# One input load of a fused attention and expert kernel moved from one DMA queue to another, another issued later

## The chip, the cores and the metric

The kernel runs on one core of a Trainium2 chip. The metric is the device time of one execution in microseconds (us); runs are compared by their medians. The profile is that of one execution; its span runs from the first to the last instruction and is shorter than the device time of the same execution.

## The reference

Two steps in a row. First an attention over 8 batches, 8 heads, 576 positions and 64 columns a head, in which each position sees itself and the 63 before it; then an expert layer with a gate, on 4608 tokens of 512 columns, with 1536 hidden columns.

```python
scores = scale * np.matmul(q, k.transpose(0, 1, 3, 2))
mask = (rel >= 0) & (rel < window)              # rel: query position less key position; window 64
scores = np.where(mask, scores, -1000000000.0)
attn = exp(scores - max) / (sum + 1e-09)
x = np.matmul(attn, v)                          # heads put side by side: 4608 x 512
gate = np.maximum(x @ w_gate, 0.0)
val = x @ w_val
out = (gate * val) @ w_out
```

Inputs and output are float32 in device memory.

## The kernel before

Everything is computed in 16-bit floats with float32 sums. Weights stay on the chip. The tokens are cut into nine tiles of 512; each tile is attended, turned so that columns lie on partitions, sent through gate and value matmuls and then through the output matmul. From the second tile on the expert products are made in Strassen's manner, with sums of weight blocks (`us`, `vs`) that VectorE and GpSimd form early in the run.

The program has two parts. `second_part` holds all but the opening. It is laid out by a planner (`Plan`), which gives each operation a key and estimated costs and writes one fixed order of instructions for each engine when the program is built; on the chip nothing is reordered. The planner's numbers, its assumed start times of the engines among them, are constants in the code. `first_part` is written out by hand. It brings the first windows of batch 0 through attention and starts the weights. The engines run in parallel, each in its own order, and wait for one another by semaphores.

What the opening does, in its order:

- Batch 0's q and k are loaded in four pieces, each of four heads: `heads_of(b, name, hh)` is the view with 128 rows (4 heads x 32 row groups) of 1152 values, `hh` 0 or 1 the half of the heads. "First" below means `hh` = 0, "second" `hh` = 1.
- First k and first q come as float32 over SyncE's DMA queue (L452, in the page `q1 hardware_dynamic`) into scratch that later holds `vs` (L450). They are then rounded to 16 bits into `nat[name, 0]` by `rounded` (L473 to L475): half of the columns by VectorE, half by ScalarE.
- Second k and second q come over GpSimd's DMA queue (`qk_load`, L386; in the page `q0 software_dynamic`), which rounds in flight: source float32, destination 16 bits.
- GpSimd then builds an identity and the band mask (`bands`, L356 to L368: two memsets, four selects), and issues three loads of v (`v_load`, L395) and four of weights (`w_part`, L376), all over q0. Later it copies parts of v (L512) and goes on with weights.
- VectorE fills constants, makes the additive `bias` from the mask (L471), and turns each of the four pieces into `kT` or `qT` by a transpose of 32x32 blocks (`qk_trans`, L392), in the order first k, first q, second k, second q. Then it copies parts of v (L512), takes reciprocals (L532), norms (L437) and turns (L442) the first tokens into `xt`.
- TensorE runs `PADS` small matmuls on zeros (L463), moves the mask into the score banks (L481, L487), one filler on zeros (`keep_hot`, L492), the scores of the first heads (L424), two more fillers, the scores of the second heads, the values (L430), and then the first expert matmuls (L836), which belong to `second_part`. ScalarE takes the exponentials (L504).

Of the kernel before, what the change touches and what calls it, by code (L numbers as in the profile page):

```python
# [10 lines left out]
FP32 = mybir.dt.float32  # L11
# [283 lines left out]
def kernel(  # L295
# [10 lines left out]
    nc = tc.nc  # L306
# [24 lines left out]
    def sb(name, shape, dt=FP16):  # L331
        return persist.tile([128] + shape, dt, name=name)

    wg, wv, wo = sb("wg", [NC, DF]), sb("wv", [NC, DF]), sb("wo", [NF, DM])
    us, vs = sb("us", [4, 2, 128 * HF]), sb("vs", [4, 2, 128 * HF])
# [3 lines left out]
    nat = {(name, hh): sb(f"{name}{hh}", [S // 32 * D]) for name in "kq" for hh in range(2)}  # L339
# [16 lines left out]
    def bands():  # L356
        nc.gpsimd.memset(mask, 1.0)
        nc.gpsimd.memset(ident, 1.0)
        for band, lo, hi in ((ident, 0, 0), (mask, 64, -1)):
            n = band.shape[1]  # L360
            nc.gpsimd.affine_select(
                out=band, in_=band, compare_op=mybir.AluOpType.is_ge, fill=0.0,
                base=lo, pattern=[[1, n]], channel_multiplier=-1,
            )
            nc.gpsimd.affine_select(
                out=band, in_=band, compare_op=mybir.AluOpType.is_ge, fill=0.0,
                base=hi, pattern=[[-1, n]], channel_multiplier=1,
            )  # L368

    def v_fixed(i, eng):  # L370
        eng.memset(v16s[i][:, :, :, D:VW].bitcast(FP32), ONE_ONE)
        eng.memset(v16s[i][0:64, 0].bitcast(FP32), 0.0)

    def w_part(wt, src, f0, f1, a):
        ns = slice(128 * f0, 128 * f1)
        nc.gpsimd.dma_start(wt[:, 2 * a:2 * a + 2, ns], src.rearrange("(a p e) n -> a p e n", a=2, e=2)[a, :, :, ns])  # L376
# [4 lines left out]
    def heads_of(b, name, hh):  # L381
        src = (q if name == "q" else k)[b, G * hh:G * hh + G]
        return src.rearrange("h (i j) d -> (h i) (j d)", i=32)

    def qk_load(b, name, hh):
        nc.gpsimd.dma_start(nat[name, hh], heads_of(b, name, hh))  # L386

    def qk_trans(b, name, hh):
        src = nat[name, hh].bitcast(FP32).rearrange("p (j e) -> p j e", e=32)
        dst = qTs[b % 2][:, hh] if name == "q" else kTs[b % 2][:, hh, 64:64 + S]  # L390
        dst = dst.bitcast(FP32).rearrange("p c o -> p (c o)")
        nc.vector.transpose(dst.rearrange("p (i j) -> p j i", i=32), src)  # L392

    def v_load(b, g, lo, hi):
        nc.gpsimd.dma_start(v16s[b % 2][lo:hi, g, :, 0:64],  # L395
                            v[b, :, 64 * g - 64 + lo:64 * g - 64 + hi].rearrange("h p d -> p h d"))

    def v_rows(b, uu):
        t = v16s[b % 2]
        up = {0: (0, 3), 1: (4, 5), 2: (6, 7)}[uu]  # L400
        down = {0: (2, 3), 1: (4, 5), 2: (6, 9)}[uu]
        return ((t[64:128, up[0]:up[1]:2], t[0:64, up[0] + 1:up[1] + 1:2]),
                (t[0:64, down[0]:down[1]:2], t[64:128, down[0] - 1:down[1] - 1:2]))
# [29 lines left out]
    def blocks_of(to, n):  # L433
        return to[:, 0:n * VW].rearrange("p (s c) -> p s c", c=VW)
# [12 lines left out]
    def first_part():  # L447

        n = S // 32 * D
        t32 = {name: vs.rearrange("p a k n -> p (a k n)").bitcast(FP32)[:, n * i:n * i + n] for i, name in enumerate("kq")}  # L450
        for name in "kq":
            nc.sync.dma_start(t32[name], heads_of(0, name, 0))  # L452
        for name in "kq":
            qk_load(0, name, 1)
        nc.vector.memset(zero, 0.0)
        nc.vector.memset(warm, 0.0)
        nc.scalar.activation(warm[:, 1:2], warm[:, 0:1], ACT.Exp)
        for i in range(2):
            v_fixed(i, nc.vector)
        nc.vector.memset(zero32, 0.0)  # L460
        bands()
        for _ in range(PADS):
            nc.tensor.matmul(banks[5][0:32, 0:16], zero[0:32, 0:32], zero[0:32, 0:16], start=True, stop=True, skip_group_check=True)  # L463
        for part in ((1, 0, 128), (3, 0, 128), (5, 0, 128)):
            v_load(0, *part)
        for a in range(2):
            for wt, src in ((wg, moe_w_gate), (wv, moe_w_val)):
                w_part(wt, src, 0, 4, a)
        for kT in kTs:
            nc.vector.memset(kT[:, :, 0:64], 0.0)  # L470
        nc.vector.tensor_scalar(bias, mask, 30000.0, -30000.0, MUL, ADD)  # L471

        def rounded(name, first, second):  # L473
            for i, copy in enumerate((first, second)):
                copy(nat[name, 0][:, n // 2 * i:n // 2 * (i + 1)], t32[name][:, n // 2 * i:n // 2 * (i + 1)])  # L475

        st = banks[0:4], banks[4:8]
        rounded("k", nc.vector.tensor_copy, nc.scalar.copy)
        for s in range(2):
            for g in range(G):  # L480
                nc.tensor.matmul(banks[6 + s][32 * g:32 * g + 32, 0:128], bias[:, 32 * s:32 * s + 32], ident,  # L481
                                 start=True, stop=True, skip_group_check=True)
        for s in range(2):
            nc.scalar.copy(biasT[:, s], banks[6 + s][:, 0:128])
        for u in range(2):
            for g in range(G):
                nc.tensor.matmul(st[u][g][:, 0:2 * U].rearrange("p (n c) -> p n c", c=64), ident,  # L487
                                 bias[:, None, :].to_broadcast([128, 2 * UB, 64]),
                                 start=True, stop=False, skip_group_check=True)

        def keep_hot(to):
            nc.tensor.matmul(to, zero32[:, 0:128], zero32[:, 0:2 * U], start=False, stop=False, skip_group_check=True)  # L492

        keep_hot(st[1][3][:, 0:2 * U])
        qk_trans(0, "k", 0)
        rounded("q", nc.scalar.copy, nc.vector.tensor_copy)
        qk_trans(0, "q", 0)
        for name in "kq":
            qk_trans(0, name, 1)
        for hh in range(2):  # L500
            for u in range(2):
                score_run([x[:, U * hh:] for x in st[u]], [(w, hh) for w in range(UB * u, UB * u + UB)], True)
                for g in range(G):
                    nc.scalar.activation(ps[4 * u + g][:, UB * hh:UB * hh + UB].rearrange("p n c -> p (n c)"),  # L504
                                         st[u][g][:, U * hh:U * hh + U], ACT.Exp, scale=scale)
            if hh == 0:
                for _ in range(2):
                    keep_hot(st[0][0][:, 0:2 * U])

        def copies(uu, copy, h0, h1):  # L510
            for to, at in v_rows(0, uu):
                copy(to[:, :, h0:h1, 0:64], at[:, :, h0:h1, 0:64])  # L512

        def values(u, hh):
            for i in range(UB):
                for s in range(2):
                    value_block(banks[2 * u + hh], VW * (2 * i + s), ps[4 * u:4 * u + 4], UB * u + i, hh, UB * hh + i, s)

        for hh in range(2):
            copies(0, nc.vector.tensor_copy, G * hh, G * hh + G)  # L520
            values(0, hh)
        nc.tensor.matmul(banks[2], zero[:, 0:128], zero, start=True, stop=True, skip_group_check=True)
        copies(1, nc.gpsimd.tensor_copy, 0, H)
        for hh in range(2):
            values(1, hh)
        SB = 2 * UB

        def x_of(u, hh):
            return xw[:, SB * (2 * u + hh):SB * (2 * u + hh) + SB]

        def recip(u, hh):
            nc.vector.reciprocal(rw[u][:, SB * hh:SB * hh + SB], blocks_of(banks[2 * u + hh], SB)[:, :, D:D + 1])  # L532

        def norm_of(u, hh):
            norm(banks[2 * u + hh], SB, x_of(u, hh), rw[u][:, SB * hh:SB * hh + SB])

        recip(0, 0)
        norm_of(0, 0)
        turn(xs[0], 0, 0, x_of(0, 0))
        recip(0, 1)  # L540
        norm_of(0, 1)
        for hh in (1, 0):
            recip(1, hh)
        for s in range(SB):
            nc.scalar.activation(x_of(1, 1)[:, s], blocks_of(banks[3], SB)[:, s, 0:D].rearrange("p (c e) -> p e c", e=2),
                                 ACT.Copy, scale=rw[1][:, SB + s])
        turn(xs[0], 1, 0, x_of(0, 1))
        norm_of(1, 0)
        for hh in range(2):
            turn(xs[0], hh, U, x_of(1, hh))  # L550
# [621 lines left out]
    with tc.manual_schedule():  # L1172
        first_part()
        PLANS.append(second_part())
# [30 lines left out]
```

## Time and profile before

| | |
|---|---|
| median of 3 runs | 307.1 us (304.96, 307.1, 308.22) |
| profiled execution, device time | 305.09 us |
| its span | 303.1 us |
| mean granted TensorE clock | 0.997 |
| busy: TensorE, VectorE, ScalarE, GpSimd | 294.5, 252.6, 213.1, 231.5 us |
| moved over q0 (GpSimd's DMA queue) | 18.29 MB, 46672 packets, 51.6% of the 16 DMA engines' span |
| moved over q1 (SyncE's and others' DMA queue) | 13.80 MB, 12720 packets, 14.5% |

The busy share of each engine in 40 slices of 7.6 us (a digit is tenths) shows how TensorE is less than full only in the first two slices and the last:

```profile
PE   7799999999999999999999999999999999999994
POOL 8698757999997999799558976699559567948630
DMA  7999999992599916933979835343931112001024
```

In names of the page PE is TensorE, PEld its weight loads, DVE VectorE, ACT ScalarE, POOL GpSimd, SP SyncE. The opening on GpSimd, in order of time (start, length, operation; an arrow in brackets names the idle time before and what ended it):

```profile
1.32 0.75 POOL L386 DMA_DIRECT2D k<-in_k_dram  x1 [0.80 <-POOLq L1189]
2.05 0.55 POOL L386 DMA_DIRECT2D q<-in_q_dram  x1
2.59 0.18 POOL L357 MEMSET mask<- 128x64 f16 x1
...
3.89 0.24 POOL L365 TENSOR_SCALAR_AFFINE_SELECT mask<-mask 128x64 f16<-128x64 f16 x1
4.07 2.80 POOL L395 DMA_DIRECT2D v<-in_v_dram  x3
6.85 0.70 POOL L376 DMA_DIRECT2D wg<-in_moe_w_gate_dram  x1
```

A DMA's row on an engine is the issue alone; the data lands later. The time to landing is listed for each issue in another view, from the issue's start.

### The profile page before, as it was taken

The numbers are of one execution on the slowest core, as the hardware profiler recorded it, in microseconds if no ns is written. First come the engines' busy times: TensorE is split into PE (matmuls) and PEld (weight loads), VectorE is DVE, ScalarE is ACT, GpSimd is POOL, SyncE is SP. The second block draws the span as 40 slices with busy tenths as digits, with TensorE's granted clock in tenths as the row PEclk, the third lists the DMA queues.
The fourth block names the chain that finished last, engine by engine and source line by source line (L and its number), as shares of the span: only waits on it lengthen the run. The fifth ranks groups of instructions, "written<-read, shape, count | busy, mean of one in ns | idle before, by whom it ended". The sixth has DMA issues, their size and how long they took to land.

```text
span 303.1 us, 11292 instructions
## 1 busy us (share of the span) xinstructions
PE 294.5 (97%) x4793; PEld 242.5 (80%) x4793; DVE 252.6 (83%) x428; ACT 213.1 (70%) x415; POOL 231.5 (76%) x233
## 2 busy tenths in 40 slices
PE   7799999999999999999999999999999999999994
PEld 5576655778767888888888888888888888888884
DVE  5879999999967988998869998889978688776962
ACT  4464426898588788785866987977588858887731
POOL 8698757999997999799558976699559567948630
PEclk9999999999999999999999999999999999999998
DMA  7999999992599916933979835343931112001024
GB/s 216 186 190 205 196 193 218 182 200 44 37 151 155 165 45 83 145 41 53 207 167 114 116 54 98 76 86 36 118 92 38 40 37 69 2 0 37 19 75 151
DMA packets 59586, 32.87 MB, mean 108 GB/s; under 512 B 39440, under 2 KB 54416, under 8 KB 59536
## 3 DMA queue, kind: packets, MB, share of 16 engines
q0 software_dynamic: 46672, 18.29, 51.6%
q1 hardware_dynamic: 12720, 13.80, 14.5%
q8 instruction: 37, 0.61, 0.9%
q14 instruction: 13, 0.11, 0.1%
q10 hardware_dynamic: 144, 0.07, 0.1%
HBM read 37.75 MB, written 9.44 MB: 156 GB/s over the span
## 4 chain that ended last, share of the span: by engine, by line
PE 89%; DMA 7%; DVE 1%; issue 1%; POOL 1%; ACT 0%; SPq 0%; ACTq 0%; DVEq 0%; POOLq 0%
PE bank L924 46%; PE bank L1088 21%; PE bank L998 6%; PE bank L789 5%; PE bank L430 4%; DMA q<-in_q_dram 3%; PE bank L424 2%; DMA v<-in_v_dram 2%; PE bank L836 2%; DMA v<-v 2%; PE bank L416 2%; DVE qT L392 0%; DVE v L512 0%; POOL k L386 0%; POOL v L395 0%
## 5 line engine op out<-in xcount | busy, mean ns | idle before, releaser
L958 POOL TENSOR_TENSOR g_sb<-pr,pr 128x512 f16<-128x512 f32 x96 | 121.1, 1277 | 37.8 <-ACT pr L949 9.1
L940 DVE TENSOR_TENSOR pr<-bank,pr 128x512 f32<-128x512 f32 x144 | 92.4, 680 | 20.2 <-PE bank L924 15.1
L933 ACT COPY pr<-bank 128x512 f32<-128x512 f32 x144 | 80.8, 590 | 23.1 <-PE bank L924 20.6
L924 PE MATMUL bank<-xt,us 128*128 128x256 f16 x384 | 56.1, 273 | 0.1
L924 PE MATMUL bank<-xt,vs 128*128 128x256 f16 x384 | 55.7, 273 | 0.0
L949 ACT ACTIVATE pr<-pr 128x512 f32<-128x512 f32 x72 | 44.9, 638 | 4.7 <-DVE pr L940 4.5
L684 ACT ACTIVATE p<-bank 128x512 f16<-128x512 f32 (+1 forms) x68 | 36.4, 591 | 10.0 <-PE bank L424 9.9
L924 PE MATMUL bank<-xt,wg 128*128 128x256 f16 x288 | 42.8, 273 | 0.1
L924 PE MATMUL bank<-xt,wv 128*128 128x256 f16 x288 | 42.8, 273 | 0.0
L924 PEld LDWEIGHTS <-vs 128*128 128x128 f16 x384 | 37.3, 98 | 5.3
L924 PEld LDWEIGHTS <-us 128*128 128x128 f16 x384 | 36.8, 98 | 5.1 <-issue 0.3
L395 POOL DMA_DIRECT2D v<-in_v_dram x40 | 35.1, 881 | 1.5 <-DMA wo<-in_moe_w_out_dram 1.1
L1088 PEld LDWEIGHTS <-g_sb 128*128 128x128 f16 x336 | 32.5, 98 | 3.9
L1088 PE MATMUL bank<-wo,g_sb 128*128 128x256 f16 x252 | 32.6, 273 | 0.0
L971 ACT ACTIVATE pr<-bank 128x512 f32<-128x512 f32 x48 | 27.5, 602 | 6.1 <-PE bank L924 4.8
L924 PEld LDWEIGHTS <-wv 128*128 128x128 f16 x288 | 27.7, 98 | 4.5
L924 PEld LDWEIGHTS <-wg 128*128 128x128 f16 x288 | 27.7, 98 | 4.1 <-DVE xt L442 0.4
L437 DVE TENSOR_TENSOR xw<-bank,r 128x448 f16<-128x448 f32 (+2 forms) x45 | 25.8, 574 | 1.6
L1088 PEld LDWEIGHTS <-ss 128*128 128x128 f16 x252 | 24.5, 98 | 3.0
L442 DVE STREAM_TRANSPOSE xt<-xw 128x512 f16<-128x512 f16 (+2 forms) x38 | 24.9, 669 | 0.4
L998 PE MATMUL bank<-wo,g_sb 128*128 128x512 f16 x96 | 23.9, 380 | 0.0
L1088 PE MATMUL bank<-ts,ss 128*128 128x256 f16 x168 | 21.8, 273 | 0.0
(103 smaller groups left out, 388.3 us busy)
## 6 DMA issues: line engine op xcount, KB each, us to landing
out_dram<-pr SPq DMA_DIRECT2D x35, 256.0 KB, 2.8
k<-in_k_dram POOLq DMA_DIRECT2D x15, 288.0 KB, 6.5
q<-in_q_dram POOLq DMA_DIRECT2D x15, 288.0 KB, 6.9
v<-in_v_dram POOLq DMA_DIRECT2D x32, 128.0 KB, 5.3
v<-v SPq DMA_DIRECT2D x12, 132.0 KB, 2.7
v<-v SPq DMA_DIRECT2D x24, 66.0 KB, 3.4
wg<-in_moe_w_gate_dram POOLq DMA_DIRECT2D x6, 256.0 KB, 6.6
wv<-in_moe_w_val_dram POOLq DMA_DIRECT2D x6, 256.0 KB, 8.7
```

The lines of the kernel that those rows point to most:

```text
L395: nc.gpsimd.dma_start(v16s[b % 2][lo:hi, g, :, 0:64], v[b, :, 64 * g - 64 + lo:64 * g - 64 + hi].rearrange("h p d -> p h d"))
L437: nc.vector.tensor_tensor(x, blocks_of(to, n)[:, :, 0:D].rearrange("p s (c e) -> p s e c", e=2), r[:, :, :, None].to_broadcast([128, n, 2, ...
L442: nc.vector.transpose(xt[:, 2 * hh:2 * hh + 2, c0:c0 + n].rearrange("p e (s c) -> p s e c", c=32), x)
L684: nc.scalar.activation(pp[g][:, 0:n].rearrange("p n c -> p (n c)"), st[g][:, 0:64 * n], ACT.Exp, scale=scale)
L924: nc.tensor.matmul(slot[to][:, HT * m:HT * m + HT], w[:, kk, 128 * m:128 * m + 128], x[:, kk], start=(first and m == 0 and kk == 0), stop= ...
L933: lambda e, hold=hold, slot=slot: nc.scalar.copy(hold["x"], slot["A"]),
L940: nc.vector.tensor_tensor(hold["x"], slot[to], hold["x"], ADD)
L949: lambda e: nc.scalar.activation(hold["x"], hold["x"], ACT.Relu), after=[o])
L958: lambda e: VEC[e].tensor_tensor(gh[:, fs:fs + 2, h], pair(a["x"]), pair(b["x"]), MUL),
L971: lambda e, hold=hold, slot=slot, i=i: nc.scalar.activation(hold["x"], slot["A"], ACT.Copy if i else ACT.Relu),
L998: nc.tensor.matmul(bank["b"][:, 0:c1 - c0], gs[t % 2][:, f, 128 * sub:128 * sub + 128], wo[:, f, c0:c1], start=(j == 0 and i == 0), stop=( ...
L1088: nc.tensor.matmul(bank[to][:, HD * m:HD * m + HD], a[:, f, 128 * m:128 * m + 128], b[:, f], start=(first and m == 0 and f == 0), stop=(f ...
```

## The change

First q no longer goes over SyncE's queue as float32 and through the rounding on VectorE and ScalarE. GpSimd loads it with `qk_load(0, "q", 0)`, straight into `nat["q", 0]` in 16 bits, as its first load, ahead of second k. The load of second q, `qk_load(0, "q", 1)`, is issued by GpSimd behind the six instructions of `bands` instead of ahead of them, still before the v loads. First k is loaded and rounded as before, without the helper. Planner, constants and `second_part` are the same.

```diff
     def first_part():
 
         n = S // 32 * D
-        t32 = {name: vs.rearrange("p a k n -> p (a k n)").bitcast(FP32)[:, n * i:n * i + n] for i, name in enumerate("kq")}
-        for name in "kq":
-            nc.sync.dma_start(t32[name], heads_of(0, name, 0))
-        for name in "kq":
-            qk_load(0, name, 1)
+        k32 = vs.rearrange("p a k n -> p (a k n)").bitcast(FP32)[:, 0:n]
+        nc.sync.dma_start(k32, heads_of(0, "k", 0))
+        qk_load(0, "q", 0)
+        qk_load(0, "k", 1)
         nc.vector.memset(zero, 0.0)
...
         nc.vector.memset(zero32, 0.0)
         bands()
+        qk_load(0, "q", 1)
...
-        def rounded(name, first, second):
-            for i, copy in enumerate((first, second)):
-                copy(nat[name, 0][:, n // 2 * i:n // 2 * (i + 1)], t32[name][:, n // 2 * i:n // 2 * (i + 1)])
-
         st = banks[0:4], banks[4:8]
-        rounded("k", nc.vector.tensor_copy, nc.scalar.copy)
+        for i, copy in enumerate((nc.vector.tensor_copy, nc.scalar.copy)):
+            copy(nat["k", 0][:, n // 2 * i:n // 2 * (i + 1)], k32[:, n // 2 * i:n // 2 * (i + 1)])
...
         qk_trans(0, "k", 0)
-        rounded("q", nc.scalar.copy, nc.vector.tensor_copy)
         qk_trans(0, "q", 0)
```

## The prediction

> **What bounds the kernel now.** I read the page first: TensorE is busy for 294.5 of 303.1 us, so it is the bound, and only its idle time can move the end. Stretches of 8 us put that idle time in two places: 2.15 us (0 to 8) and 1.64 us (8 to 16) before the first expert matmuls, then 0.69 us (40 to 48), 0.17 (48 to 56), 0.09 (64 to 72) and nothing until the last stores. The change edits only the part before 14.5 us, so I followed the chain of waits there:
>
> ```profile
> 1.32 0.74 POOL k L386
> 2.05 8.29 DMA q<-in_q_dram
> 10.35 0.02 issue
> 10.37 1.26 DVE qT L392
> ...
> 11.70 0.29 DVE v L512
> ...
> 13.84 0.59 DVE xt L442
> 14.43 0.04 issue
> 14.47 1.48 PE bank L836 x16
> ```
>
> Columns: start, length, what. The opening ends last on the load of the second q (issued 2.05, landed 10.35), its transpose, the copies of v, norm and turn. From 14.47 TensorE hardly stops, so a shift of that point shifts the end. I then asked how the four loads share the transfer engines, by the queue table of two windows (packets, MB, share of 16 engines), 2 to 5 us and 5.2 to 7.9 us:
>
> ```profile
> q1 hardware_dynamic: 233, 1.00, 93.9%
> ```
>
> ```profile
> q0 software_dynamic: 241, 0.52, 104.5%
> q1 hardware_dynamic: 24, 0.06, 5.6%
> ```
>
> First SP's queue q1 (k and q as f32) has the engines alone, then Pool's q0 takes over without a gap. Issue start plus time to landing gives k first heads 0.82+4.2 = 5.02, q first 1.26+5.1 = 6.36, k second 1.32+6.5 = 7.82, q second 2.05+8.3 = 10.35, the three v parts 4.07+7.0 = 11.07, 4.99+6.6 = 11.59 and about 12.24 (Pool's copy begins at 12.27). So this is one stream, and the loads land in order, about 1.4 us each. The last takes 2.5; the window 8 to 9.1 us shows what came between:
>
> ```profile
> q0 software_dynamic: 959, 0.16, 188.6%
> q8 instruction: 1, 0.02, 5.1%
> ```
>
> One instruction packet holds 5.1% of 16 engines for 1.1 us, so one engine for 0.9 us. The DVE timeline (start, length) shows where compute meets the stream:
>
> ```profile
> 6.86 0.45 DVE L475 CAST q<-vs 128x576 f16<-128x576 f32 x1
> 7.41 1.26 DVE L392 STREAM_TRANSPOSE qT<-q 128x576 f32<-128x576 f32 x1
> 8.52 1.24 DVE L392 STREAM_TRANSPOSE kT<-k 128x576 f32<-128x576 f32 x1
> 10.37 1.26 DVE L392 STREAM_TRANSPOSE qT<-q 128x576 f32<-128x576 f32 x1 [0.62 <-DMA q<-in_q_dram]
> ```
>
> DVE already waits 0.62 us for the stream before the last transpose. Further on the stream touches TensorE again (list of TensorE's weight-load waits: us in total, times, longest):
>
> ```profile
> PEld L789 <- DMA wv<-in_moe_w_val_dram: 0.3, 1, 0.3
> ...
> PEld L836 <- DMA wg<-in_moe_w_gate_dram: 0.3, 1, 0.3
> ```
>
> The weights arrive just in time, so a later stream is a later end, one for one.
>
> **The change, part by part.**
>
> *Rounding of q removed.* ACT loses 0.67 us (6.43 to 7.10): its next work is the first exponential at 9.13, after a wait of 2.02 for TensorE, so this is worth nothing by itself. DVE loses 0.45: the first q transpose can follow the first k transpose at about 7.05 instead of 7.41, the first scores start at 8.36 instead of 8.72, and the second k transpose ends 0.36 earlier. There the gain ends: the last transpose waits for the second q, and DVE's idle 0.62 becomes about 1.0. Worth 0 while that load lands near 10.4; without that cover it would be -0.36.
>
> *SP's second issue removed* (0.42 us). SP does nothing more until the store at 50.35: 0.
>
> *First q through Pool.* Same bytes read, half written. Price from two stretches of one us: 429 GB/s written by f32 packets (4 to 5 us, so 429 read), 208 GB/s written by rounding packets (7 to 8 us, so 416 read). 589.8 kB take 1.375 or 1.418 us: +0.04 in the stream. Measured landings bound it: 6.36-5.02 = 1.34 for f32 against 7.82-6.36 = 1.46 rounded, +0.12. I take +0.1. Pool issues it where it issued the second k before (1.32, 0.75 long, the first one's length), so k second takes the slot at 2.07, and the masks keep their 2.59 to 4.13.
>
> When do its packets begin? Before, none of q0 moved until about 5.1, as q1 had the engines. The nearest row with idle engines is the k load issued at 69.19, whose first bytes move at 70.48, 1.3 us later; with the first issue 0.15 longer that makes 2.8. The last of the first k's packets begin by about 4.3, 0.7 before it lands, so the queue would be ready in time: the low end is a gap of 0. The high end is 5.1, the earliest that the trace shows for this place: one more load stands behind 5.1 than before, +1.4. I take 2.8, since issue length plus 0.7 us also fits v loads on idle engines (74.00: 0.95 long, first bytes 1.66 after). The Trainium skill, "DMA: Bandwidth & Descriptors", section "Queues, rings and completion order", says that an engine takes turns between its queue rows, packet by packet. By that rule the missing q0 packets before 5.1 mean that they were not ready, and the sum would be the +1.4. The trace speaks more for order of arrival: the store issued at 97.96 behind Pool's backlog took 5.7 us to land, against a median of 2.8.
>
> *Second q behind the masks.* Its issue moves from 2.05 to 4.07 (0.55 long). Ready 0.7 after its end, 5.3, while the stream frees for it only about 7.5 (0.35 before k second lands, 7.86): 2.2 us of cover. On Pool it is moved past memsets and selects, which do not slip, as two issues still precede them; but three v issues and four weight issues behind it slip by 0.55. The third v is issued by 7.4, ready 8.1, needed some 0.6 (v spacing) twice after the second q's bytes, not before 9.5. The last weight issue ends at 10.2 instead of 9.64, where Pool waits 2.63 us for v anyway. All hidden; with the cover gone at most 0.55. DVE needs the mask as before (4.16).
>
> *The sum.* k first 5.02, q first 6.46, k second 7.92, q second 10.45 (the instruction packet still ahead of its end), v parts 11.17 and 11.69. Last transpose 10.47 to 11.73, copies 11.80, first expert matmuls 14.57: **+0.1 us**, and the weights that end TensorE's waits at 15.97 and 18.27 are as much later. Span 303.2; outside the span lie 305.09-303.1 = 1.99, so 305.2 for the profiled execution. That run stands 2.0 below the median of 307.1 (runs 304.96 to 308.22); on the median the forecast is 307.2.
>
> **The rivals.**
>
> *Late first packets (slower).* Place: the engines between the end of k first, about 4.3, and the first rounding packet. From 4.3 on every us costs one, up to +1.4: 308.5. For it: no q0 packet before 5.1. Against: 1.3 us on idle engines, and the queued store. 0.17.
>
> *A slower TensorE clock (slower).* The first scores and the two L492 fillers come 0.36 earlier, the second scores do not, so TensorE's gap between them grows from 0.62 to about 1.1 us. In this trace 128x384 matmuls take 0.34 us at 4.7 to 7.5 (8 in 2.74) and 0.17 at 20.8 (32 in 5.37), with a granted clock of 1.00 in both rows. If the gap brings the slow pace back for such a 2.74 us stretch, 1.4 us of matmuls go missing, and some 0.6 in the values before it: +2.0, 309.2. It decides only if a gap near 1.1 suffices; 0.89 at 3.51 was followed by the slow pace, but so was everything at the start. The Trainium skill, "TensorE: Matmul & The Clock Gate", Part 1, asks for an idle window of about 3.4 us, which speaks against it. 0.07.
>
> *The engines fill up (faster).* Between 2.8 and 4 us they write 240 to 332 GB/s where 429 is possible; if rounding packets use that room, 0.3 us are gained: 306.9. Before, waiting packets did not use it. 0.10.
>
> *No effect:* the order of landings, and all that hangs on it, is what it was: 307.1. 0.06.
>
> *The written order stumbles (slower).* Everything behind 14.5 runs in a fixed order. TensorE's longest stall there is 0.69 us at 43.17 (values behind a Pool copy of v, L655, behind a load issue). If a shifted Pool queue brings such a stall in six of the remaining tiles, +4: 311. For it: Pool is 76% busy and its transfers end many waits; against: the shift is 0.1 us and TensorE does not wait at all from 72 on. 0.10.
>
> **How the numbers follow.** The forecast has 0.50: 307.2. The range must hold late packets (308.5), the clock (309.2) and the scatter of before, -2.1 to +1.1 around its median; it leaves out the stumble and the outer scatter: 304.9 to 309.6. 1% is 3.07 us, about what a measurement can tell from no change. No case but the stumble passes that bound alone. Slower by more: stumble 0.09, late packets with scatter 0.06, clock 0.03, forecast with scatter 0.04: 0.22. Faster by more: forecast 0.07, engines filled 0.04, no effect 0.01, and 0.01 from the stumble's mirror, a stall that vanishes: 0.13. Same: 0.65.
>
> **What would show it.** Right: rounding packets right behind k first (by 4.4), q first landed near 6.5, the first scores near 8.4, DVE idle about 1.0 before the last transpose, its start at 10.4 to 10.6, first L836 matmul near 14.6. Late packets: no q0 packets until 5, first L836 near 15.9. Clock: L836 matmuls of 192 columns above the 0.09 us apart of now. The forecast falls if first L836 moves by over 0.5 us, or if TensorE's waits behind 20 us grow.

## The result, and the profile after

| | before | after |
|---|---|---|
| median of the paired runs | 305.31 us (22 runs) | 306.56 us (22 runs) |
| profiled execution, device time | 305.09 us | 307.66 us |
| its span | 303.1 us | 305.9 us |
| busy: TensorE, VectorE, ScalarE, GpSimd | 294.5, 252.6, 213.1, 231.5 us | 296.3, 252.5, 212.5, 231.7 us |

The ratio after to before is 1.0045, with a 95% interval of 1.0027 to 1.0064: the change costs 1.4 us, 0.8 to 2.0. The ratio leaves out the runs in a slower state, which the medians in the table count. The kernel after is slower, by less than 1%. The profiled execution of the kernel after is 1.1 us above the median of its own runs, so the difference of the two spans, 2.8, overstates the change.

Two places tell where it went. The first is the list in order of time (start, length, engine, line, operation; in brackets the idle time before and what ended it) of the kernel after:

```profile
5.26 1.26 DVE L392 STREAM_TRANSPOSE kT<-k 128x576 f32<-128x576 f32 x1 [0.24 <-ACT k L475]
...
8.05 1.26 DVE L392 STREAM_TRANSPOSE qT<-q 128x576 f32<-128x576 f32 x1 [1.53 <-DMA q<-in_q_dram]
...
9.36 0.83 PE L424 MATMUL bank<-qT,kT 32*128 32x64 f16 x48 [0.60 <-DVE qT L392]
...
9.46 1.26 DVE L392 STREAM_TRANSPOSE kT<-k 128x576 f32<-128x576 f32 x1
...
10.26 2.93 PE L489 MATMUL bank<-zero 128*128 128x384 f32 x4
...
11.94 1.26 DVE L392 STREAM_TRANSPOSE qT<-q 128x576 f32<-128x576 f32 x1 [1.22 <-DMA q<-in_q_dram]
...
13.68 1.58 DVE L508 COPY v<-v 64x512 f16<-64x512 f16 x4 [0.48 <-DMA v<-in_v_dram]
...
14.57 1.27 POOL L508 COPY v<-v 64x512 f16<-64x512 f16 x2 [4.15 <-DMA v<-in_v_dram]
...
16.62 0.82 PE L832 MATMUL bank<-xt,wg 128*128 128x192 f16 x8 [0.24 <-DVE xt L442]
```

VectorE now waits three times for the stream of loads: 1.53 us for the first q, 1.22 for the second, 0.48 for v; before it was 0.62 once. The transpose of the second q starts at 11.94 instead of 10.37, the first expert matmul (L832 here) at 16.62 instead of 14.47. By issue start plus time to landing, first q lands at 8.02 (before 6.36), second k at 9.46 (7.82), second q at 11.87 (10.35), the v parts at 12.73, about 13.65 and 14.43 (11.07, 11.59, about 12.24). Only first k is earlier, 4.52 for 5.02.

The chain of waits (start, length, what) says the same from the end: it now runs over the third part of v, which is the last of the late stream, and no longer over the second q.

```profile
4.63 1.76 POOL v L395 x2
6.40 8.03 DMA v<-in_v_dram
14.42 0.02 issue
...
14.57 0.60 POOL v L508
```

The second place is the engines that carry the loads. The queue tables of the window 3.6 to 6 us (packets, MB, share of 16 engines), first of before, then of after:

```profile
DMA packets 250, 0.86 MB, mean 358 GB/s; under 512 B 31, under 2 KB 31, under 8 KB 250
...
q1 hardware_dynamic: 185, 0.71, 72.2%
q0 software_dynamic: 65, 0.15, 33.5%
```

```profile
DMA packets 114, 0.23 MB, mean 97 GB/s; under 512 B 16, under 2 KB 16, under 8 KB 114
...
q0 software_dynamic: 102, 0.22, 67.5%
q1 hardware_dynamic: 12, 0.01, 1.6%
```

Before, SP's second float32 load fills this window and Pool's queue follows it: 65 packets hold 33.5% of the engines. After, Pool's queue has the engines nearly alone and moves 102 packets, which hold 67.5% of them. So it moves little, and a packet lasts longer: 67.5% of 16 engines for 2.4 us is 25.9 us for 102 packets, 0.25 us each, against 12.9 for 65, 0.20; and a third of the engine time is idle. The packets' own records show the rest. After, the first rounding packet begins at 3.52, right behind first k, and in steps of half a us from 3.5 on there begin 10, 17, 20, 26, 24, 32, 37, 27, 26 of 2304 bytes, and 41 and 46 only from 8.0 on; sixteen of them last 0.4 to 1.4 us, where 0.19 is usual. Before, the first begins at 5.1, the steps from 5.0 on are 22, 43, 42, 42, 43, 47, and no packet lasts 0.4. Each load leaves sixteen updates of its semaphore, as many as there are engines, and counts as landed with the last. After, those of first q come between 5.46 and 8.03, half of them by 6.8; before, those of second k, the first load of Pool's queue there, come between 6.87 and 7.85. So some engines are through early, and the late ones set the landing.

Of the 2.15 us at the first expert matmul, 1.52 are there when the second q lands. The other 0.6 comes between: the values wait for the late v (13.68 and 14.57 above). Behind 16 us TensorE's idle time grows a little too. Three stretches of the kernel after (bounds, length, busy time of TensorE with its count, then weight loads, VectorE, ScalarE and GpSimd, the granted clock, DMA share, GB/s):

```profile
16.00:24.00 8.00, 7.55 (x160) 6.65 (x148) 6.11 (x15) 4.04 (x13) 7.93 (x11) 1.00 1.17 175
24.00:32.00 8.00, 7.70 (x82) 4.55 (x81) 6.93 (x21) 3.96 (x10) 6.00 (x9) 1.00 1.40 201
...
40.00:48.00 8.00, 6.85 (x112) 4.55 (x110) 7.04 (x14) 1.86 (x3) 4.07 (x6) 1.00 1.53 194
```

TensorE is idle there for 0.45, 0.30 and 1.15 us, where before it was 0.01, 0 and 0.69. Of the 0.45, 0.24 is still the wait before the first expert matmul at 16.62; the longest wait, for the copy of v near 43 us, is 1.1 instead of 0.7. This part differs from profile to profile, as the runs show.

### The profile page after: what moved, and what is told of

Same layout as the page of the kernel before. It is cut to its first block, busy times and chain, and to the rows that moved or that the text cites. A ratio compares the mean times of both kernels' runs of the same rounds, so it can differ in the third digit from the quotient of the medians.

```text
span 305.9 us, 11287 instructions
## 1 busy us (share of the span) xinstructions
PE 296.3 (97%) x4793; PEld 243.5 (80%) x4793; DVE 252.5 (83%) x427; ACT 212.5 (69%) x414; POOL 231.7 (76%) x234
## 4 chain that ended last, share of the span: by engine, by line
PE 82%; DMA 9%; POOL 5%; issue 1%; DVE 1%; ACT 0%; POOLq 0%; ACTq 0%; DVEq 0%
PE bank L920 48%; PE bank L1084 21%; DMA v<-in_v_dram 6%; PE bank L994 5%; PE bank L430 4%; DMA wv<-in_moe_w_val_dram 3%; PE bank L424 3%; POOL v L395 2%; PE bank L416 2%; POOL wg L376 1%; DVE kT L392 0%; POOL q L386 0%; POOL v L508 0%; POOL xt L751 0%; POOL vs L869 0%
## 5 line engine op out<-in xcount | busy, mean ns | idle before, releaser
L392 DVE STREAM_TRANSPOSE qT<-q 128x576 f32<-128x576 f32 x16 | 19.9, 1245 | 3.2 <-DMA q<-in_q_dram 3.2
```

## The experiments

The question was why loads over Pool's queue, which landed 1.46 us apart before, take so much longer when one of the two float32 loads ahead of them is gone. The table gives, from each run's profile, the landings (where no row gives one, the start of the next instruction) and the start of the first expert matmul; the ratio is to the runs of the kernel before on the same chip, whose medians were 305.1 to 305.7 us. "One run" is a single time, which can't tell 1.4 us from nothing.

| run | first q | second k | second q | first expert matmul | ratio, 95% interval |
|---|---|---|---|---|---|
| before | 6.36 | 7.82 | 10.35 | 14.47 | 1 |
| after | 8.02 | 9.46 | 11.87 | 16.62 | 1.0045 (1.0027 to 1.0064) |
| e1_again | 8.2 | 9.65 | 11.97 | 16.75 | 1.0035 (1.0009 to 1.0061) |
| e2_queue_only | 8.42 | 9.9 | 11.30 | 15.79 | 1.0048 (1.0031 to 1.0065) |
| e3_masks_only | 6.25 | 8.02 | 10.1 | 14.74 | 0.9999 (0.9983 to 1.0015) |
| e4_shadow | 7.62 | 10.26 | 11.1 | 15.82 | 1.0050 (1.0015 to 1.0085) |
| e5_pool_pause | 8.4 | 9.85 | 12.25 | 16.94 | one run: 307.3 us |
| e6_no_fills | 8.2 | 9.56 | 11.87 | 16.79 | 1.0056 (1.0015 to 1.0097) |
| e7_warm_first | 9.45 | 10.9 | 12.3 | 17.00 | one run: 308.5 us |
| e8_all_pool | 7.1 | 8.7 | 10.50 | 15.14 | 1.0037 (0.9996 to 1.0077) |
| e9_all_behind | 8.27 | 9.7 | 11.2 | 16.36 | 1.0041 (1.0014 to 1.0067) |
| e10_pool_plain | 6.84 | 8.88 | 11.0 | 15.63 | 1.0034 (1.0001 to 1.0067) |
| e11_gap | 7.76 | 11.44 | 12.80 | 17.75 | one run: 308.8 us |
| e12_k_over_sp | 7.5 | 5.96 | 10.13 | 15.31 | 1.0004 (0.9977 to 1.0032) |

The first expert matmul of one profile and the ratio of all runs don't go strictly together: e8 has 15.14 and 1.0037, e12 has 15.31 and 1.0004, and their intervals overlap.

The diffs stand against the kernel after, if nothing else is said.

### The change again, and its two halves

e1_again is the kernel after, unchanged.

> The changed kernel once more. Theory A (slow start of Pool's queue: with only one float32 load in front, the rounding packets begin ragged and at half pace): first q again lands near 8.0 instead of 6.4, second q near 11.9, first L832 matmul between 15.7 and 16.7, ratio to before 1.003 to 1.007. Theory B (second q behind the masks is what came late) and theory C (the first run's profile was a bad draw) differ in where: by B the first q lands near 6.5 and only second q and v are late; by C first L832 near 14.6 and ratio 1.000 to 1.002.

Its opening repeats the first profile within 0.2 us. But the four filler matmuls behind the first scores are faster here (list in order of time of e1_again):

```profile
10.32 1.56 PE L489 MATMUL bank<-zero 128*128 128x384 f32 x4 [0.24 <-ACT p L500]
...
13.33 0.55 PE L424 MATMUL bank<-qT,kT 32*128 32x64 f16 x48 [1.46 <-DVE qT L392]
```

1.56 us instead of 2.93, and TensorE then waits 1.46 for the second q. So the slow fillers of the first profile only filled a wait.

e2_queue_only keeps first q on Pool's queue, but issues the second q ahead of the masks:

```diff
         qk_load(0, "k", 1)
+        qk_load(0, "q", 1)
...
         bands()
-        qk_load(0, "q", 1)
```

> First q over Pool's queue, second q issued ahead of the masks as before. Theory A: nothing is cured, first q lands near 8, the start of the expert matmuls stays 1.2 to 2.2 us later than before, ratio 1.003 to 1.007; the masks end 0.55 later, hidden. Theory B: back to before, expert matmuls start near 14.6, ratio 1.000 to 1.002.

e3_masks_only is the other half, the kernel before with one line moved:

```diff
-        for name in "kq":
-            qk_load(0, name, 1)
+        qk_load(0, "k", 1)
...
         bands()
+        qk_load(0, "q", 1)
```

> First q over SP as float32 with its rounding, as before; only second q's issue moved behind the masks. Theory A: as before, second q lands near 10.4 and the expert matmuls start between 14.4 and 14.8, ratio 0.999 to 1.001. Theory B: 15.5 to 16.6, ratio 1.003 to 1.007.

The two halves are as far apart as before and after. With the queue move alone the first q is as late as after and the ratio is the same (VectorE's list in order of time of e2_queue_only):

```profile
8.48 1.25 DVE L392 STREAM_TRANSPOSE qT<-q 128x576 f32<-128x576 f32 x1 [1.86 <-DMA q<-in_q_dram]
...
11.34 1.26 DVE L392 STREAM_TRANSPOSE qT<-q 128x576 f32<-128x576 f32 x1
```

With the second q behind the masks alone, the ratio is 0.9999, and the last transposes stand about where they stood before (the same list of e3_masks_only):

```profile
8.38 1.24 DVE L392 STREAM_TRANSPOSE kT<-k 128x576 f32<-128x576 f32 x1
10.11 1.26 DVE L392 STREAM_TRANSPOSE qT<-q 128x576 f32<-128x576 f32 x1 [0.49 <-DMA q<-in_q_dram]
```

The cover that the prediction gave this step, 2.2 us, held. In total time, all of the cost that the runs can tell is the move of first q to the other queue. In the opening the two parts do interact: with the queue move but without the later issue (e2) the second q lands 0.6 and the first expert matmul starts 0.8 earlier than after, and no gain of it shows in the ratio.

### The old load put back beside the new one

e4_shadow adds SP's old float32 load of first q to the kernel after. Nothing reads what it loads:

```diff
         nc.sync.dma_start(k32, heads_of(0, "k", 0))
+        q32 = vs.rearrange("p a k n -> p (a k n)").bitcast(FP32)[:, n:2 * n]
+        nc.sync.dma_start(q32, heads_of(0, "q", 0))
```

> The changed kernel plus SP's old float32 load of first q into scratch that nobody reads: one load more (2.4 MB read becomes 3.0), whose only use is to keep the engines busy until 5.1 while Pool's queue gets ready. Theory A: rounding packets begin at 5.1 at full pace, three loads of 1.45 us follow: first q lands near 7.8, second k near 9.3, second q near 10.7 plus the instruction packet's 0.9 = 11.6, so the extra load is for free: expert matmuls start 15.5 to 16.4, within 0.3 us of the changed kernel's own, ratio 1.002 to 1.006. If the engines were simply full in the changed kernel, the extra load costs its 1.4 us on top: start near 18, ratio 1.008 to 1.012.

Queue table of e4_shadow, 3.6 to 6 us:

```profile
DMA packets 238, 0.80 MB, mean 335 GB/s; under 512 B 25, under 2 KB 25, under 8 KB 238
...
q1 hardware_dynamic: 161, 0.63, 64.0%
q0 software_dynamic: 77, 0.18, 41.4%
```

VectorE's list of e4_shadow:

```profile
7.65 1.25 DVE L392 STREAM_TRANSPOSE qT<-q 128x576 f32<-128x576 f32 x1 [0.47 <-DMA q<-in_q_dram]
```

With 0.59 MB more to read, the first q lands 0.4 us earlier than after, second k 0.8 later, the second q 0.8 earlier, and the first expert matmul starts 0.8 earlier. Pool's packets begin at 4.83, near the full pace at once (34, 37, 42, 44 in the half-us steps from 5.0 on), and none of them lasts 0.4 us. The whole run is no faster, though. The profiled execution took 313.03 us, 6.2 more than the median of its runs, so only its opening is read; the granted clock there was 0.50 from 15.3 to 18.7. Why the ratio kept the loss is not shown.

### Three other explanations

*Pool's issues disturb its own first loads, or come too late.* e5_pool_pause puts a fill of scratch between the masks and the second q, so that everything behind it on Pool is issued later still:

```diff
         bands()
+        nc.gpsimd.memset(gs[1][:, 0:6], 0.0)
         qk_load(0, "q", 1)
```

> The changed kernel with a useless fill of 3072 columns on GpSimd between the masks and second q's issue, so that GpSimd issues no transfer from 2.6 us until 6 us or later. Only the first two loads of Pool's queue are looked at. If GpSimd's issuing of q and v from 4.07 on disturbs the rounding packets of the first loads (theory D), first q lands near 6.5 and second k near 8.0. If the start of the queue itself is slow (theory A), first q lands between 7.5 and 8.4 again and second k between 9.2 and 10. The whole kernel is slower by the pause, 2 to 4 us, in both.

The fill takes 2.66 us (4.08 to 6.74), and the second q is issued at 6.67 instead of 4.07. It lands 0.4 later, and the first expert matmul starts 0.3 later. Pool's queue has a backlog, and in this range the time of the issue does not set the landing. First q and second k land at 8.4 and 9.85 although Pool issues nothing between 2.6 and 6.67, so its further issues aren't what delays them. Beside the fill VectorE is slow too: its step for `bias` takes 2.60 us instead of 0.18, and first k's transpose begins at 7.18.

*VectorE's fills, which run from 0.94 to 2.95 us, hold up what Pool prepares for its loads.* e6_no_fills moves one of them behind the mask's way into the banks and the rest behind the first k transpose; between 1.2 and 4.1 VectorE then does nothing:

```diff
-        for i in range(2):
-            v_fixed(i, nc.vector)
-        nc.vector.memset(zero32, 0.0)
...
-        for kT in kTs:
-            nc.vector.memset(kT[:, :, 0:64], 0.0)
...
+        nc.vector.memset(zero32, 0.0)
...
+        for kT in kTs:
+            nc.vector.memset(kT[:, :, 0:64], 0.0)
+        for i in range(2):
+            v_fixed(i, nc.vector)
```

> The changed kernel with VectorE's fills of v, zero32 and kT taken out of 1.2 to 3.0 us, where GpSimd issues the first loads, and put behind the first k rounding and transpose. If VectorE's fills hold up the making of the first transfers' descriptors (theory E), first q lands near 6.5, the expert matmuls start near 14.6 and the ratio is 1.000 to 1.002. By theory A nothing changes: first q near 8, start 15.5 to 16.8, ratio 1.003 to 1.008.

Landings and ratio are those of the kernel after.

*The first use of the queue is slow.* e7_warm_first sends a tiny rounding load, 128x32, ahead of the others:

```diff
         nc.sync.dma_start(k32, heads_of(0, "k", 0))
+        nc.gpsimd.dma_start(gs[1][:, 0, 0:32], heads_of(0, "q", 0)[:, 0:32])
         qk_load(0, "q", 0)
```

> The changed kernel with one tiny rounding load (128 rows of 32 values, into scratch) ahead of first q on Pool's queue. If only the very first transfer of the queue is slow (theory F: first use), it takes the blow, and first q lands by 6.7. If it is each start on engines that have no backlog (theory A), first q lands near 8 or later again, and second k near 9.5 to 10.

The tiny load lands at 4.81, and first q later than ever (VectorE's list in order of time of e7_warm_first):

```profile
9.46 1.25 DVE L392 STREAM_TRANSPOSE qT<-q 128x576 f32<-128x576 f32 x1 [2.86 <-DMA q<-in_q_dram]
```

This is not the plain miss that it seems. By the packets' records 15 of the 16 engines were done with it by about 6.2, and 15 of its 16 updates had come by 6.46, where the kernel after had seven; one engine alone kept it to 9.45. A packet of 1.88 us (5.80 to 7.68) fits that engine, though the records name none. So in this one run most engines did what theory F expects, and the landing did not; whether the first use of the queue has a part is open.

### No float32 load at all

e8_all_pool loads first k over Pool's queue too, rounded on the way:

```diff
-        k32 = vs.rearrange("p a k n -> p (a k n)").bitcast(FP32)[:, 0:n]
-        nc.sync.dma_start(k32, heads_of(0, "k", 0))
+        qk_load(0, "k", 0)
...
-        for i, copy in enumerate((nc.vector.tensor_copy, nc.scalar.copy)):
-            copy(nat["k", 0][:, n // 2 * i:n // 2 * (i + 1)], k32[:, n // 2 * i:n // 2 * (i + 1)])
```

> The change carried further: first k too comes rounded over Pool's queue, no float32 load at all. By pace alone (four loads of 1.45 us from 2.8 us on, instruction packet 0.9) second q would land near 9.9 and the expert matmuls start by 14.3, ratio 0.998 to 1.000. By theory A the engines stand empty while the queue starts: first k lands after 6, second q near 11.5 to 13, expert matmuls start 15.5 to 17.5, ratio 1.003 to 1.010.

If Pool's queue were slow on idle engines as such, this would be the worst case. It is better than the kernel after. Queue table of e8_all_pool, 3.6 to 6 us:

```profile
DMA packets 224, 0.46 MB, mean 192 GB/s; under 512 B 24, under 2 KB 24, under 8 KB 224
...
q0 software_dynamic: 224, 0.46, 107.4%
```

Alone on the engines, Pool's queue moves 224 packets in the window in which it moved 102 after. It begins at 2.78 and is at its full pace from 4.5 on (14, 29, 39, 30, 46, 47, 45 in the half-us steps from 2.5 on), with twelve packets of 0.4 to 1.1 us before 4.0. First k lands at 5.7, 2.9 us after its first packet, so a start on idle engines isn't free either; first q, behind it on the same queue, lands at 7.1, 0.9 earlier than after. With the second q at 10.50 and the start at 15.14 neither expectation was met. The total stays between before and after; its interval holds 1.

### Later issue, no rounding, a gap

e9_all_behind issues all three loads of q and k on Pool behind the masks, the first at 2.27 instead of 1.32:

```diff
-        qk_load(0, "q", 0)
-        qk_load(0, "k", 1)
...
         bands()
+        qk_load(0, "q", 0)
+        qk_load(0, "k", 1)
         qk_load(0, "q", 1)
```

> The changed kernel with all three of Pool's q and k loads issued behind the masks, so that first q's packets can be ready only when first k's float32 packets are over (near 4.0 instead of 2.8). Theory G (hand-over: rounding packets that come up while the engines are still full of a float32 load stumble when that load ends 0.7 us later; they do not when they come to idle engines, as with all loads over Pool, or 2.3 us or more before its end, as in the kernel before): issued some 1.3 us later, first q lands earlier than the 8.0 of the changed kernel, 6.9 to 7.6, and the expert matmuls start 15.0 to 15.9. If the delay is only a matter of how early Pool's queue is asked (theory A as first stated), first q lands near 9.3, the start is 17 or later and the ratio above 1.006.

It met neither expectation in full. Issued 0.95 later, first q lands 0.25 later, and the second q 0.6 earlier than after. The pace is still thin (7, 15, 25, 30, 38 in the half-us steps). Here 14 of the 16 updates of first q had come by 6.92, and the last two came at 8.19 and 8.27. An instruction packet, which holds one engine, ran from 6.09 to 6.98; it may account for one of the two, but the records name no engine.

e10_pool_plain loads first q over Pool's queue as plain float32 and rounds it on ScalarE and VectorE, as before the change. Against the kernel before:

```diff
-        for name in "kq":
-            nc.sync.dma_start(t32[name], heads_of(0, name, 0))
-        for name in "kq":
-            qk_load(0, name, 1)
+        nc.sync.dma_start(t32["k"], heads_of(0, "k", 0))
+        nc.gpsimd.dma_start(t32["q"], heads_of(0, "q", 0))
+        qk_load(0, "k", 1)
...
         bands()
+        qk_load(0, "q", 1)
```

> The changed kernel's order of transfers, but first q comes over Pool's queue as plain float32 into the old scratch and is rounded by ScalarE and VectorE as before. If the rounding in flight is what is slow at first (theory H), first q lands by 6.5 and the expert matmuls start near 14.6 to 15. If it is the hand-over between the queues (theory G), whatever the packets carry, first q lands between 7.4 and 8.5 and the start is 15.5 to 16.8, ratio 1.003 to 1.008.

First q lands at 6.84, 1.2 earlier than after; the second at 11.0, 0.65 later than before. Long packets are there too, among the plain ones of 4608 bytes and the rounding ones behind them. Landing and start lie between the two expectations, 6.84 near the one and 15.63 in the other. So the rounding may be a part of it, and the queue without rounding has the trouble as well.

e11_gap is e9_all_behind with a further fill on Pool, so that the engines lie idle between SP's load and Pool's first packet:

```diff
         bands()
+        nc.gpsimd.memset(gs[1][:, 0:3], 0.0)
         qk_load(0, "q", 0)
```

> As the run with all of Pool's loads behind the masks, with a fill of 1536 columns on GpSimd ahead of them, so that first q's packets are ready near 5.0 and the engines stand empty from 3.8 until then. One look at the stream, not at the whole time. Theory G (only the hand-over hurts; idle engines start Pool's queue well): about 43 packets per 0.5 us within 1 us of the first one, first q lands 3 us after its first packet, near 8.1, second q near 11.2, so no later than in the changed kernel although all is issued 2.3 us later. If the float32 load in front hurts however long it is over, the pace stays at 20 to 35 per 0.5 us for 3 to 4 us, first q lands after 9 and second q after 12.8.

Here the first q lands 2.75 us after its first packet (5.045), against 4.5 after. But then the stream turns thin, 25 to 31 packets per half us from 7.0 to 9.5, and second k takes the delay (VectorE's list of e11_gap):

```profile
7.76 1.26 DVE L392 STREAM_TRANSPOSE qT<-q 128x576 f32<-128x576 f32 x1 [1.27 <-DMA q<-in_q_dram]
11.45 1.26 DVE L392 STREAM_TRANSPOSE kT<-k 128x576 f32<-128x576 f32 x1 [2.43 <-DMA k<-in_k_dram]
```

The first half is what theory G expects, the second is not. So it is not the hand-over from SP's queue to Pool's alone, nor the time of the issue alone.

### Two float32 loads in front, and first q still on Pool's queue

e12_k_over_sp keeps the new way of first q and the new place of second q, and sends both pieces of k over SP as float32, with the rounding on VectorE and ScalarE:

```diff
-        k32 = vs.rearrange("p a k n -> p (a k n)").bitcast(FP32)[:, 0:n]
-        nc.sync.dma_start(k32, heads_of(0, "k", 0))
+        t32 = [vs.rearrange("p a k n -> p (a k n)").bitcast(FP32)[:, n * i:n * i + n] for i in range(2)]
+        for hh in range(2):
+            nc.sync.dma_start(t32[hh], heads_of(0, "k", hh))
         qk_load(0, "q", 0)
-        qk_load(0, "k", 1)
...
+        rounded(0, nc.vector.tensor_copy, nc.scalar.copy)
...
+        rounded(1, nc.scalar.copy, nc.vector.tensor_copy)
```

> The change with its cover given back: both k loads come over SP as float32 and are rounded by ScalarE and VectorE, both q loads come rounded over Pool's queue, second q issued behind the masks. Two float32 loads in front, as in the kernel before, but first q does go over Pool. Theory G: no stumble; first q lands near 7.8, second q 10.1 to 10.5, expert matmuls start 14.3 to 15.0, ratio 0.998 to 1.002. If first q over Pool's queue, or its being asked so early, is what costs, the start is 15.5 or later and the ratio 1.003 to 1.007.

The loss is gone: 305.65 us, ratio 1.0004 (0.9977 to 1.0032). VectorE's list and the queue table (3.6 to 6 us) of e12_k_over_sp:

```profile
7.51 1.26 DVE L392 STREAM_TRANSPOSE qT<-q 128x576 f32<-128x576 f32 x1 [0.47 <-DMA q<-in_q_dram]
...
10.15 1.25 DVE L392 STREAM_TRANSPOSE qT<-q 128x576 f32<-128x576 f32 x1 [0.30 <-DMA q<-in_q_dram]
```

```profile
q1 hardware_dynamic: 161, 0.61, 63.2%
q0 software_dynamic: 75, 0.17, 41.7%
```

First q again goes over Pool's queue and is rounded on the way, and its packets begin at 5.0, with 32, 43, 42 and 40 in the first steps. What differs from the kernel after is that two float32 loads go ahead of them instead of one, and that second k (landed at 5.96) no longer goes over Pool's queue. The first expert matmul, at 15.31 between the two expectations, is still 0.84 later than before in this profile, because the v copies waited; no version here is shown to beat the kernel before.

### What the set shows, and what stays open

With two float32 loads on SP's queue ahead (before, e3, e4, e12), Pool's queue runs near its full pace from its first packets, at 4.8 to 5.1 us. With one (after, e1, e2, e5, e6, e7, e9, e10, e11) it has thinner stretches of 2 to 4.5 us, and the second q is 0.65 to 2.45 us later than before. Packets of 0.4 us and more among the q and k loads number 0, 4, 0 and 6 in the first group, 16 to 28 in the second.

Shown is that a second float32 load ahead brings Pool's first packets to full pace: e4 is the kernel after with that load and nothing else. In the opening it is worth more than its own time; in total time e12 shows the gain and e4 does not. Excluded as the only cause are the place of the masks, the time at which Pool issues, VectorE's fills and the rounding. Idle engines are a part of the cost, not all of it: on idle engines a load takes 2.7 to 2.9 us from first packet to landing (e8, e11), behind a single float32 load 4.5 (after).

Not shown is what makes the packets of Pool's queue long and sparse: whether the engines wait for their next piece of work or for the memory behind it. A rival that no run tests alone is the time that Pool's queue has before it may begin. From its first issue to its first packet 3.5 to 3.8 us pass with two loads ahead, and 1.5 to 2.3 in all the others. That e8, with 1.5, does better than after, with 2.2, speaks against it in part.

## Why the prediction was right and where it failed

*Right: the range, the direction, and what bounds the opening.* The time came inside the range and slower, by less than 1%. The stream of loads sets the opening; neither the slow fillers (e1) nor VectorE's fills (e6) move the first expert matmul. The rest was luck. The forecast of 307.2 stood on a median of three runs, 307.1, which 22 runs put at 305.31, and its difference was +0.1 where +1.4 was measured: a level too high and a difference too small cancel in part, and the range, wide for the scatter and the rivals, held the result. By its own signs the forecast's case fell. It was to fall if the first expert matmul moved by over 0.5 us, and that moved by 2.15; first q was to land near 6.5 and landed at 8.02, the first scores near 8.4 began at 9.36, the last transpose, due at 10.4 to 10.6, at 11.94. Only the first sign held, rounding packets right behind first k.

*Wrong: the term "First q through Pool", "I take +0.1".* It was priced by stretches at 7 to 8 us, where the rounding packets already ran behind two float32 loads, and by the landings of the same stretch, 1.46 us for a load. In its new place the load took 4.5 us from its first packet (3.52) to its landing (8.02), 1.66 later than the float32 load it replaced. At the second q +1.52 is left in the profile, +0.95 in e2, which has this step alone. A row of the trace of before hinted at it, and was used for its first byte only: the load of k issued at 69.19 on engines that had nothing else to do. The window 69 to 75 us of before, in 40 slices and by issue (KB, us to landing):

```profile
GB/s 0 0 0 0 0 0 0 0 0 46 138 92 15 92 169 184 230 200 184 215 230 92 140 15 15 15 0 0 0 0 0 0 0 0 0 0 0 0 0 0
...
k<-in_k_dram POOLq DMA_DIRECT2D x1, 288.0 KB, 4.2
```

A first packet at 70.48 and a landing at 73.4 are 2.9 us, twice the 1.46, with a thin start (15 to 169 GB/s in the first six slices that move anything) and a thin end at 15. Six of its first eight packets last 0.4 to 0.8 us. Counted from 4.3, where the forecast let Pool's packets begin, this would have put first q at 7.2, 0.8 above the 6.36 of before: an estimate from that row, and half of the 1.66 that came. Counted from 3.52, where they did begin, it gives 6.4, so this row does not account for the 4.5 us either.

*The rival "late first packets" had the size, +1.4, and the wrong mechanism.* Its sign, no packet of Pool's queue until 5, did not come: they began at 3.52, behind first k, as the forecast said. And readiness was as forecast: in e8_all_pool they begin at 2.78, where the text took 2.8. They were not late but slow. A third case, "on time, at half pace", was missing.

*The rule set beside it.* The Trainium skill, "DMA: Bandwidth & Descriptors", section "Queues, rings and completion order", has an engine alternate between its queue rows packet by packet. Pool's packets, ready at 2.78 in e8_all_pool, moved only at 5.1 in the kernel before and at 4.83 in e4_shadow, as SP's two loads were running out, and none moved between those two. Here the measurement does not agree with the rule. Order of arrival, for which the text decided, fits; a fixed precedence of SP's queue would fit as well.

*Second q behind the masks, "All hidden".* Right where it stood, behind two float32 loads: e3_masks_only, ratio 0.9999 (0.9983 to 1.0015). Behind the thin stream it was not all hidden: without it (e2) the second q lands 0.6 earlier than after, near the 0.55 that the text allows with the cover gone. Pool's queue had one new wait, 0.37 us before a weight issue at 9.72; Pool waits 4.15 for v behind it anyway.

*"Rounding of q removed … Worth 0".* No run isolates it, and the waits now around it are longer than what it gives. Its side effect went the other way: with the load this late the first scores began at 9.36, not 8.36, and VectorE's idle time before the last transpose became 1.22 behind another 1.53, where the text gave about 1.0 in all.

*"The weights arrive just in time, so a later stream is a later end, one for one".* Only roughly. From the first expert matmul to the end of the span it is 288.6 us before, 289.3 after, 288.9 in e12, 288.4 in e9 and 288.1 in e6: part of a delay is taken up by the wait for v near 43 us, or added to there (0.7 us before, 1.1 after, 0.3 in e12, e9 and e6). This may be why +2.15 in one profile is +1.4 in the runs.

*A slower clock.* It does not part the kernels. Of the 20 runs of the kernel after that the ratio counts, seven have a mean granted clock of 0.994 or less and a median of 306.6 us, thirteen have 0.997 or more and 306.5. e12_k_over_sp has a clock of 0.50 from 15.1 to 18.5 without a loss in the runs. The prediction's reading of this rival has an error: the 1.00 that it gives beside the slow 128x384 matmuls at 4.7 to 7.5 us is no measured clock, since the clock records of that trace begin only at 7.7 us. The fillers show what the missing record stands for. The four of them take 1.56 us where records of 1.00 have begun (before, e1 and eight more), 2.92 or 2.93 where none has (after, first record at 13.6 us; e9, 15.4; e11, 13.0), and 1.95 in e5, where the first record begins in the midst of them, at 12.9.

*Engines that fill up* did not come; they emptied. *The written order* did not stumble: TensorE's waits behind 20 us grew by some tenths.

## What to carry to other kernels

The price of a transfer that is moved to another queue is read from a row with the same surroundings, what goes ahead of it on the engines and how long the queue has run, not from the middle of a running stream. A load that looks superfluous can be the cover under which another queue gets going: the test is to put it back beside the new way (e4_shadow) or to put another one in its place (e12_k_over_sp). And a change of several parts is settled soonest by running each part alone: e2 and e3 had placed the cost in two runs.

## What the runs showed of the hardware that was not expected

- Pool's queue, behind two float32 loads, began about 43 packets of 2304 bytes per half us; behind a single load it began 10 to 37 for up to 4.5 us (after), with 16 to 28 packets that last 0.4 to 1.9 us instead of 0.19. Idle engines have such packets at the start as well (e8, and the load of 69.19 in the kernel before).
- One late engine decides a landing: in e7_warm_first 15 engines were done by about 6.2 us, the load at 9.45.
- GpSimd's queue was ready 1.5 us after its first issue (e8), and waited until 5.1 us behind two loads on SP's queue (before).
- TensorE runs at half its pace until the first clock record of 1.00, which begins between 7.7 us (before) and 15.4 us (e9). The tables print 1.00 there because nothing is recorded. In e1, e4, e6, e11 and e12 a stretch of 0.50 follows later, each 3.4 us long. What sets the times was not tried.
